# A two-stage kernel: q and k loaded by token, v's overlaps copied on chip, weights decoded two steps later

## The chip, the cores and the metric

The kernel runs on one core of one Trainium2 chip. The metric is the device time of one execution, in microseconds (us). The names used are TensorE (PE, with PEld for its weight loads), VectorE (DVE), ScalarE (ACT), GpSimd (POOL) and SyncE (SP, which issues all DMAs here).

## The reference, cut to what matters

```
attention, per batch and head (2 batches, 8 heads, 576 tokens, 64 wide, float32):
    scores = q @ k^T / 8
    heads 0-3: keep key j for query i if 0 <= i - j < 32
    heads 4-7: keep it if 0 <= i - j < 128 and (i - j) % 4 == 0
    attn = exp(scores - max) / (sum + 1e-9);  y = attn @ v
x = y as 1152 tokens x 512
x = mish(x @ w_in) @ w_out                          # 512 -> 2048 -> 512
out = sum over 4 experts e of p_e * (relu(x @ w1[e]) @ w2[e])   # 512 -> 1024 -> 512
```

## The kernel before, in words

**Units and steps.** The attention is cut into ten units, each a batch and a chunk of 128 tokens (the fifth chunk of a batch has 64), with all eight heads. `att_step(s)` (line 437) is a software pipeline over them: in step s it works on unit s+2 (`transposes`), s+1 (`spread`), s (`scores`, `softmax`, `probsT`), s-1 (`probsT_copy`, `values`, `sums`, `normalise`) and s-2 (`xT`, `x_hi`, `x_lo`). The schedule is manual: each engine runs its instructions in the order in which this function issues them, and so does SP with its DMAs. Steps run from -2 to 9.

**A unit's way.** `load_qk` (line 306) puts two tokens, 512 contiguous bytes, on a partition: the k of a unit on the first 64 partitions, the q on the other 64, one DMA each. `transposes` turns each head's block (line 320); `spread` (line 323) is eight ScalarE copies of 64 lanes x 256 that sort heads and even and odd tokens into `qkP` (heads 0 to 3) and `qkD` (heads 4 to 7). In these tiles k stands as head pairs: head j of a pair on partitions 64j to 64j+63, with zeros in the other half, so that one product gives the scores of two heads. `scores` adds the mask with a product of `sel` and `msk` and then runs products for 32 queries at a time (line 351) or for every fourth token (line 355). `softmax` is the row maximum `mx` (line 363), the subtraction `pr` (364) on VectorE and exp (365) on ScalarE; `sums` (369 to 371) are the row sums and their reciprocal; `normalise` (401) scales the outcome of `values` into `xn`. `xT` turns it, and `x_hi` (420, ScalarE) and `x_lo` (424, VectorE) split it into a high and a low part, xh and xl.

**v.** `vP` and `vD` hold v with the tokens of the block before on 32 of the 64 partitions of a head and the block's own tokens on the other 32. As blocks overlap, the DMAs of `load_vP` (260) and `load_vD` (273) read nearly every token twice. GpSimd zeroes the halves that belong to the other head of a pair (`zero_v`, 202, and `zero_k`, 214), chunk by chunk.

**Weights.** w_in and w_out are float32 and are needed as a high and a low part too. They come in 32 halves: half 2u is unit u's w_in (512 columns), half 2u+1 its w_out. A half is loaded into one of three `raw` buffers (`dec_load`), and then passes through five instructions, spread over three calls: `dec_dve` (143) with number n does line 150 of half n, line 157 of half n-1 and the GpSimd subtraction of line 164, which gives the low part, of half n-2; `dec_act` (167) does the conversion of line 173 of half n, writes the high part of half n-1 (line 179) and then counts n up. The first four units go to `wxh` and `wxl`, the others to the `late` tiles. In the attention steps there is one pair of calls per step, from `DEC0` on:

```
        if DEC0 <= s < NA:
            dec_act()
        if DEC0 - 4 <= s < DEC0 - 1:
            dec_load()
        if DEC0 - 1 <= s < NA:
            dec_dve()
```

After step 9 come two more `dec_act` and one `dec_dve`, written out by hand (lines 793 to 813), and then each of the steps 2 to 15 of the first matrix stage has two pairs (`step1_act`, 769).

**The matrix stages.** In stage one, step i multiplies the first 512 tokens by unit i of w_in (`first`, line 497, 12 products: per 128 rows of the weights high x xh, high x xl, low x xh), applies mish, splits, and multiplies by w_out (`second`, 517). For the sixteen steps of these tokens the order on TensorE is first(i), second(i-1), first(i+1), second(i), and on ScalarE in step i mish(i), the split into gh, and then the two `dec_act`. The other tokens and the four experts follow; all their operands are there by then or prepared beside them.

Of the kernel before, what the change touches and what calls it, by code (L numbers as in the profile page):

```python
# [8 lines left out]
F32 = mybir.dt.float32  # L9
# [5 lines left out]
AF = mybir.ActivationFunctionType  # L15
# [8 lines left out]
def kernel(  # L24
# [13 lines left out]
    PE, ACT, DVE, POOL, SP = nc.tensor, nc.scalar, nc.vector, nc.gpsimd, nc.sync  # L38
    ctx.enter_context(tc.manual_schedule())

    B, H, S, D = q.shape
# [3 lines left out]
    NF1 = w_in.shape[1] // 128  # L45
    NF2 = w1.shape[2] // 128
    NUA = 4
    DEC0 = 3
    NWARM = 8

    GRP = ((0, 512), (512, 320), (832, 320))
# [11 lines left out]
    def nm(s):  # L63
        uid[0] += 1
        return f"{s}{uid[0]}"

    def bank(n):
        return ps.tile([128, 512], F32, tag=f"bank{n}", name=nm("bank"))
# [120 lines left out]
    ap1 = att.enter_context(tc.tile_pool(name="ap1", bufs=1))  # L189
    NCH = (S + 127) // 128  # L190


    qkP = ap1.tile([128, 2, 3, 32 + S], F32, name="qkP")

    qkD = ap1.tile([128, 2, 3, NCH + 1, 2, 64], F32, name="qkD")
    vP = ap1.tile([128, 2, S // 32, 2, D], F32, name="vP")
    vD = ap1.tile([128, 2, 2, NCH, 4 * D], F32, name="vD")
    ident = ap1.tile([128, 128], F32, name="ident")
# [3 lines left out]
    def zero_v(c):  # L202
        blk = slice(4 * c, min(4 * c + 4, S // 32))
        for j in range(2):
            POOL.memset(vP[64 * j:64 * j + 64, :, blk, 1 - j, :], 0.0)  # L205
            if c == 0:
                POOL.memset(vP[64 * j:64 * j + 32, :, 0, j, :], 0.0)
        if c in (0, NCH - 1):
            POOL.memset(vD[:, :, :, c], 0.0)
        else:  # L210
            for j in range(2):
                POOL.memset(vD[64 * j:64 * j + 64, :, 1 - j, c], 0.0)  # L212

    def zero_k(c, eng):
        n = min(128, S - 128 * c)
        for j in range(2):
            rows = slice(64 * j, 64 * j + 64)
            eng.memset(qkP[rows, :, 1 - j, 32 + 128 * c:32 + 128 * c + n], 0.0)
            eng.memset(qkD[rows, :, 1 - j, c + 1, :, 0:n // 2], 0.0)

    warm = ap1.tile([128, 512], BF16, name="warm")
    DVE.memset(warm, 0.0)
# [9 lines left out]
                           base=-lo, pattern=[[1, 64]], channel_multiplier=-1 if lo == 0 else 0)  # L232
    for t in sel.values():
        DVE.memset(t, 0.0)
    DVE.memset(qkP[:, :, 0:2, 0:32], 0.0)
    for p in range(2):
        DVE.memset(qkD[:, p, 0:2, 0], 0.0)
        DVE.memset(qkD[:, p, 0:2, NCH, :, (S % 128) // 2:64], 0.0)
    zero_k(0, DVE)
    zero_v(0)  # L240
    for c in range(1, NCH):
# [10 lines left out]
    t = bank(7)  # L252
# [3 lines left out]
    def msk_b(n):  # L256
        return msk.unsqueeze(1).to_broadcast([64, n, 64])


    def load_vP(b, g0, g1):  # L260

        for j in range(2):
            src = v[b, j:j + 1]
            if g0 == 0:
                SP.dma_start(out=vP[64 * j + 32:64 * j + 64, :, 0, j, :],
                             in_=bass.AP(src.tensor, src.offset, [[D, 32], [2 * S * D, 2], [1, D]]))
            g = max(g0, 1)
            for p in range(2):
                SP.dma_start(out=vP[64 * j:64 * j + 64, p, g:g1, j, :],
                             in_=bass.AP(src.tensor, src.offset + (2 * p * S + 32 * (g - 1)) * D,  # L270
                                         [[D, 64], [32 * D, g1 - g], [1, D]]))

    def load_vD(b, c0, c1):

        for j in range(2):
            src = v[b, 4 + j:5 + j]
            lo, n = 64 * j, 64
            off = src.offset + 128 * (c0 - 1) * D
            if c0 == 0:
                lo, n, off = lo + 32, 32, src.offset  # L280
            elif c1 == NCH:
                n = 32 + (S - 128 * c0) // 4
            if c1 == c0 + 1:
                SP.dma_start(out=vD[lo:lo + n, :, j, c0, :],
                             in_=bass.AP(src.tensor, off, [[4 * D, n], [2 * S * D, 2], [1, 4 * D]]))
                continue
            for p in range(2):
                SP.dma_start(out=vD[lo:lo + n, p, j, c0:c1, :],
                             in_=bass.AP(src.tensor, off + 2 * p * S * D,
                                         [[4 * D, n], [128 * D, c1 - c0], [1, 4 * D]]))  # L290


    v_loads = {-2: [(load_vD, 0, 1, NCH - 1)], -1: [(load_vP, 0, 8, S // 32), (load_vD, 0, NCH - 1, NCH)],
               2: [(load_vD, 1, 0, 1), (load_vP, 1, 0, 8)], 4: [(load_vD, 1, 1, NCH - 1)],
               5: [(load_vP, 1, 8, S // 32), (load_vD, 1, NCH - 1, NCH)]}

    class Unit:
        def __init__(self, b, c):
# [5 lines left out]
            self.tbanks, self.sbank, self.s = ((4, 5), 6, None) if second else ((0, 1), 2, None)  # L304

        def load_qk(self):

            self.nat = ap1.tile([128, H, 2 * D], F32, tag="nat", name=nm("nat"), bufs=4)
            rows = slice(128 * self.c, 128 * self.c + self.n)
            for lo, src in ((0, k), (self.n // 2, q)):  # L310
                SP.dma_start(out=self.nat[lo:lo + self.n // 2],
                             in_=src[self.b, :, rows, :].rearrange("h (t two) d -> t h (two d)", two=2))

        def transposes(self):
            n = self.n
            self.pts = []
            for g in range(2):
                pt = bank(self.tbanks[g]).rearrange("p (h t) -> p h t", h=4)
                for h in range(4):
                    PE.transpose(pt[:, h, 0:n], self.nat[0:n, 4 * g + h, :], ident[0:n, 0:n])  # L320
                self.pts.append(pt[:, :, 0:n].rearrange("p (a j) (k t) -> p a j k t", j=2, k=2))

        def spread(self):

            n, c = self.n, self.c

            def move(g, par, j):
                src = slice(64 * par, 64 * par + 64)
                dst = slice(64 * j, 64 * j + 64)
                if g == 0:  # L330
                    cols = 32 + 128 * c
                    return qkP[dst, :, j:3:2 - j, cols + par:cols + n:2], self.pts[0][src, :, j]
                return qkD[dst, :, j:3:2 - j, c + 1, par, 0:n // 2], self.pts[1][src, :, j]

            for g in range(2):
                for par in range(2):
                    for j in range(2):
                        ACT.activation(*move(g, par, j), AF.Copy)  # L338

        def scores(self):  # L340
            n, c = self.n, self.c
            self.s = s = bank(self.sbank)
            if self.first:
                PE.matmul(s[:, 0:256], sel["s"], msk_b(4), start=True, stop=False, skip_group_check=True)
                PE.matmul(s[:, 256:512], sel["f"], msk_b(4), start=False, stop=False, skip_group_check=True)
            else:
                PE.matmul(s, sel["n"], msk_b(8), start=True, stop=False, skip_group_check=True)
            for p in range(2):
                for g in range(n // 32):
                    k0 = 128 * c + 32 * g  # L350
                    PE.matmul(s[32 * g:32 * g + 32, 128 * p:128 * p + 128], qkP[:, p, 2, k0 + 32:k0 + 64],
                              qkP[:, p, 0:2, k0:k0 + 64], start=False, stop=True, skip_group_check=True)
            for p in range(2):
                for r in range(4):
                    PE.matmul(s[32 * r:32 * r + n // 4, 256 + 128 * p:384 + 128 * p],
                              qkD[:, p, 2, c + 1, r % 2, r // 2:n // 2:2],
                              qkD[:, p, 0:2, c:c + 2, r % 2, r // 2::2], start=False, stop=True, skip_group_check=True)

        def softmax(self):
            mx = ap1.tile([128, 8], F32, tag="mx", name=nm("mx"), bufs=3)  # L360
# [12 lines left out]
        def probsT(self):  # L373
            pt = bank(3).rearrange("p (s t) -> p s t", s=4)
            pr = self.pr.rearrange("p s c -> p (s c)")
            for s in range(4):
                PE.transpose(pt[:, s, :], pr[:, 128 * s:128 * s + 128], ident)
            self.pt = pt

        def probsT_copy(self):  # L380
            self.pT = ap1.tile([128, 4, 128], F32, tag="pT", name=nm("pT"), bufs=1)
            ACT.activation(self.pT, self.pt, AF.Copy)

        def values(self):
            self.x = x = bank(4).rearrange("p (s d) -> p s d", s=4)
# [41 lines left out]
    NA = len(au)  # L427
    for n in range(3):
        au[n].load_qk()
    load_vP(0, 0, 8)  # L430
    load_vD(0, 0, 1)

    def unit_at(n):
        return au[n] if 0 <= n < NA else None
# [1 line left out]
    def att_step(s, mid=None, pre=None):  # L436
        n2, n1, u, p1, p2 = (unit_at(n) for n in (s + 2, s + 1, s, s - 1, s - 2))
        if p1:
            p1.probsT_copy()
        if n1:  # L440
            n1.spread()
        if pre:
# [7 lines left out]
        if p2:  # L450
            p2.xT()
        if p1:
            p1.sums()
        if p2:
            p2.x_hi()
            p2.x_lo()
        if DEC0 <= s < NA:
            dec_act()
        if p1:
            p1.normalise()  # L460
        if n2:
            n2.transposes()
        if mid:
# [2 lines left out]
            u.probsT()  # L466
        if unit_at(s + 5):
            unit_at(s + 5).load_qk()
        for load, *args in v_loads.get(s, ()):
            load(*args)  # L470
        if DEC0 - 4 <= s < DEC0 - 1:
            dec_load()
        if DEC0 - 1 <= s < NA:
            dec_dve()

    yacc = {}

# [315 lines left out]
    u1, u2 = au[NA - 1], au[NA - 2]  # L793
    ACT.preload_act_table_set(MISH)
    u1.probsT_copy()
    u1.values()
    u2.xT()
    steps[0].act()
    u1.sums()
    dec_act()  # L800
    dec_dve()
    steps[2].first()
# [108 lines left out]
```

## Time and profile before

| | us |
|---|---|
| median of 3 runs | 670.16 |
| lowest and highest run | 669.08, 671.54 |
| the profiled execution: time | 668.4 |
| the profiled execution: span from first to last instruction | 666.6 |
| TensorE, matmuls busy | 636.1 |
| VectorE busy | 290.3 |
| ScalarE busy | 275.3 |
| GpSimd busy | 158.8 |

The time of an execution is its span and the 1.8 us around it. The attention takes the first 75 us or so, the matrix stages the rest. Busy times of different engines overlap. A row of a timeline gives the start and the duration of an instruction, its line and operation, what it writes and reads, and in brackets how long its engine was idle before it and which instruction ended that wait.

### The profile page before, as it was taken

Reading aid. Unit: us, or ns where it says so; the run is one execution under the profiler, and the core shown is the slowest. Engines: PE = TensorE matmul, PEld = TensorE weight load, DVE = VectorE, ACT = ScalarE, POOL = GpSimd, SP = SyncE. Lnnn points to the kernel's source line nnn. Section 1 sums busy time; section 2 is a strip of 40 time slices with the busy share of each in tenths; the row PEclk is TensorE's granted clock in tenths of the full one; section 3 lists DMA queues with packets and bytes.
Section 4 is the critical chain, followed back from the end, with each engine's and each line's share of the span. In section 5 each row is a group of like instructions: output and inputs, shape, how many; then the busy total and the mean of one; then the engine's idle time right before and its main releaser. Section 6 shows DMA issues by size and latency. Waiting matters only on the chain.

```text
span 666.6 us, 10149 instructions
## 1 busy us (share of the span) xinstructions
PE 636.1 (95%) x4148; PEld 564.7 (85%) x4148; DVE 290.3 (44%) x490; ACT 275.3 (41%) x553; POOL 158.8 (24%) x170
## 2 busy tenths in 40 slices
PE   7676899999999999979999999999999999999997
PEld 4455678888999999969998889998889998898986
DVE  3577876661311223345444452444632544623323
ACT  7797666662322234443244432334422344322210
POOL 8011245550300003345033410043400134300000
PEclk9998999999999999989999999999999999999999
DMA  9999356640000012222003210021210022000102
GB/s 182 221 205 206 98 160 190 188 126 0 1 1 1 1 64 64 64 63 64 1 32 94 64 64 1 0 64 64 64 63 1 1 78 85 28 1 1 63 1 79
DMA packets 47310, 45.82 MB, mean 69 GB/s; under 512 B 12192, under 2 KB 39968, under 8 KB 47264
## 3 DMA queue, kind: packets, MB, share of 16 engines
q1 hardware_dynamic: 47264, 45.18, 25.6%
q8 instruction: 32, 0.52, 0.3%
q14 instruction: 14, 0.11, 0.1%
HBM read 42.81 MB, written 2.36 MB: 68 GB/s over the span
## 4 chain that ended last, share of the span: by engine, by line
PE 86%; ACT 4%; POOL 3%; DMA 2%; DVE 2%; issue 1%; SPq 0%; POOLq 0%; ACTq 0%; DVEq 0%
PE bank L751 30%; PE bank L698 27%; PE bank L517 14%; PE bank L497 14%; DMA raw<-in_moe_w_in_dram 1%; DMA nat<-in_q_dram 1%; ACT qkD L338 1%; ACT qkP L338 1%; ACT xh L420 1%; POOL vP L205 1%; POOL vD L212 0%; PE bank L320 0%; DVE xl L424 0%; DVE scr L150 0%; ACT pr L365 0%
## 5 line engine op out<-in xcount | busy, mean ns | idle before, releaser
L698 PE MATMUL bank<-xh,late 128*128 128x256 f32 (+1 forms) x512 | 121.1, 298 | 5.0 <-ACT late L710 3.6
L698 PEld LDWEIGHTS bank<-xh,late 128*128 128x128 f32 x512 | 88.6, 188 | 9.5 <-ACT late L710 5.1
L698 PE MATMUL bank<-wxh,late 128*128 128x320 f32 (+1 forms) x384 | 95.3, 298 | 0.0
L751 PE MATMUL bank<-late,gh 128*128 128x512 f32 x288 | 89.8, 393 | 0.0
L497 PE MATMUL bank<-xh,late 128*128 128x320 f32 (+1 forms) x288 | 76.3, 338 | 0.0
L698 PE MATMUL bank<-xl,late 128*128 128x256 f32 (+1 forms) x256 | 75.5, 295 | 0.0
L517 PE MATMUL bank<-gh,late 128*128 128x320 f32 (+1 forms) x288 | 72.6, 338 | 0.0
L654 POOL TENSOR_TENSOR raw<-raw 128x256 f32<-128x256 f32 x16 | 11.7, 734 | 238.4 <-DVE late L543 238.4
L698 PEld LDWEIGHTS bank<-wxh,late 128*128 128x128 f32 x384 | 68.3, 189 | 0.0
L506 DVE TENSOR_TENSOR gl<-scr,gh 128x512 fp32r<-128x512 f32 (+1 forms) x32 | 25.0, 780 | 88.7 <-ACT gh L505 88.7
L751 PEld LDWEIGHTS bank<-late,gh 128*128 128x128 f32 x288 | 52.8, 190 | 9.7
L502 ACT ACTIVATE scr<-bank 128x320 f32<-128x320 f32 (+1 forms) x48 | 23.4, 492 | 88.1 <-PE bank L497 88.1
L716 DVE TENSOR_TENSOR raw<-bank,late 128x256 f32<-128x256 f32 (+1 forms) x32 | 14.6, 457 | 101.2 <-PE bank L698 94.1
L751 PE MATMUL bank<-late,gl 128*128 128x512 f32 x144 | 57.0, 396 | 0.0
L698 PE MATMUL bank<-wxl,late 128*128 128x256 f32 (+1 forms) x192 | 56.6, 295 | 0.0
L542 ACT ACTIVATE late<-raw 128x512 fp32r<-128x512 f32 (+1 forms) x64 | 48.2, 783 | 19.9 <-PE bank L751 16.8
L497 PEld LDWEIGHTS bank<-xh,late 128*128 128x128 f32 x288 | 50.7, 188 | 4.3
L517 PEld LDWEIGHTS bank<-gh,late 128*128 128x128 f32 x288 | 50.1, 188 | 4.2
L751 PE MATMUL bank<-late,late 128*128 128x512 f32 x216 | 52.6, 391 | 0.0
L543 POOL TENSOR_TENSOR late<-raw,late 128x1024 fp32r<-128x1024 f32 x16 | 38.7, 2419 | 57.1 <-ACT late L542 57.1
L698 PEld LDWEIGHTS bank<-xl,late 128*128 128x128 f32 x256 | 48.3, 189 | 2.5
L497 PE MATMUL bank<-xl,late 128*128 128x320 f32 (+1 forms) x144 | 48.6, 338 | 0.0
(140 smaller groups left out, 1164.1 us busy)
## 6 DMA issues: line engine op xcount, KB each, us to landing
raw<-in_moe_w_dram SPq DMA_DIRECT2D x32, 512.0 KB, 3.5
raw<-in_moe_w_in_dram SPq DMA_DIRECT2D x16, 512.0 KB, 4.1
raw<-in_moe_w_out_dram SPq DMA_DIRECT2D x16, 512.0 KB, 3.6
out_dram<-scr SPq DMA_DIRECT2D x9, 256.0 KB, 2.1
nat<-in_k_dram SPq DMA_DIRECT2D x8, 256.0 KB, 5.6
nat<-in_q_dram SPq DMA_DIRECT2D x8, 256.0 KB, 6.2
vD<-in_v_dram SPq DMA_DIRECT2D x8, 192.0 KB, 7.0
vP<-in_v_dram SPq DMA_DIRECT2D x8, 160.0 KB, 6.5
```

The costliest lines, as they stand in the source:

```text
L205: POOL.memset(vP[64 * j:64 * j + 64, :, blk, 1 - j, :], 0.0)
L338: ACT.activation(*move(g, par, j), AF.Copy)
L497: PE.matmul(h, a[:, c, :], x[:, c, :], start=c == 0 and k == 0, stop=c == 3 and k == 2)
L502: ACT.activation(self.hc[:, self.w * i:self.w * (i + 1)], h, AF.Mish)
L506: DVE.tensor_tensor(out=self.glo, in0=self.hc, in1=self.ghi.bitcast(F32), op=ALU.subtract)
L517: PE.matmul(yacc[self.grp][d], a[:, s], x[:, g], start=u == 0 and k == 0, stop=u == NF1 - 1 and k == 2)
L542: ACT.activation(hi, src, AF.Copy)
L543: eng.tensor_tensor(out=lo, in0=src, in1=hi.bitcast(F32), op=ALU.subtract)
L654: POOL.tensor_tensor(out=a22, in0=a21, in1=a22, op=ALU.add)
L698: PE.matmul(out, w, x(k), start=first and k == 0 and i == 0, stop=k == 1 and i == 2, skip_group_check=not first)
L716: DVE.tensor_tensor(out=self.cb[:, 0:N], in0=self.c, in1=p1, op=ALU.add)
L751: PE.matmul(acc, x[:, s], a[:, cols], start=self.p == 0 and f == 0 and i == 0, stop=self.p == NP2 - 1 and f == 1 and i == 2)
```

## The change

- `load_qk` puts one token to a partition: a DMA for k and one for q, each 128 partitions x 8 heads x 256 bytes. A transpose of 128 columns is then a pair of heads, in place. `spread` becomes two copies of 64 lanes x 512 for k, with the zeros beside them, and one of 128 x 512 for q. `kk` and `qq` replace `qkP` and `qkD`; the dilated heads' products read every fourth token.
- `load_v` loads only a block's own tokens; `copy_v`, on GpSimd, copies those of the block before from there, in step s for unit s. The zeroing of `vD` for the first and the last chunk is cut into smaller pieces, so as to leave the loaded partitions out. v is loaded in two DMA groups for a batch in place of four.
- `DEC0` is 5 in place of 3.
- `sums` is issued at the start of a step, right after `probsT_copy`; `normalise` ahead of `x_hi` and `x_lo`.

```diff
-    DEC0 = 3
+    DEC0 = 5
...
-    qkP = ap1.tile([128, 2, 3, 32 + S], F32, name="qkP")
-    qkD = ap1.tile([128, 2, 3, NCH + 1, 2, 64], F32, name="qkD")
+    kk = ap1.tile([128, 4, 2, 128 * (NCH + 1)], F32, name="kk")
+    qq = ap1.tile([128, 4, S], F32, name="qq")
...
     def zero_v(c):
         blk = slice(4 * c, min(4 * c + 4, S // 32))
         for j in range(2):
             POOL.memset(vP[64 * j:64 * j + 64, :, blk, 1 - j, :], 0.0)
+            POOL.memset(vD[64 * j:64 * j + 64, :, 1 - j, c], 0.0)
             if c == 0:
                 POOL.memset(vP[64 * j:64 * j + 32, :, 0, j, :], 0.0)
-        if c in (0, NCH - 1):
-            POOL.memset(vD[:, :, :, c], 0.0)
-        else:
-            for j in range(2):
-                POOL.memset(vD[64 * j:64 * j + 64, :, 1 - j, c], 0.0)
+                POOL.memset(vD[64 * j:64 * j + 32, :, j, 0], 0.0)
+            if c == NCH - 1:
+                POOL.memset(vD[64 * j + 32:64 * j + 64, :, j, c], 0.0)
     def zero_k(c, eng):
-        n = min(128, S - 128 * c)
         for j in range(2):
-            rows = slice(64 * j, 64 * j + 64)
-            eng.memset(qkP[rows, :, 1 - j, 32 + 128 * c:32 + 128 * c + n], 0.0)
-            eng.memset(qkD[rows, :, 1 - j, c + 1, :, 0:n // 2], 0.0)
+            eng.memset(kk[64 * j:64 * j + 64, :, 1 - j, 128 * c + 128:128 * c + 256], 0.0)
...
+    def load_v(b, c0, c1):
+        g0, g1 = 4 * c0, min(4 * c1, S // 32)
+        cf = min(c1, S // 128)
         for j in range(2):
+            own = slice(64 * j + 32, 64 * j + 64)
             for p in range(2):
+                src = v[b, 2 * p + j:2 * p + j + 1]
+                SP.dma_start(out=vP[own, p, g0:g1, j, :],
+                             in_=bass.AP(src.tensor, src.offset + 32 * g0 * D, [[D, 32], [32 * D, g1 - g0], [1, D]]))
+            src = v[b, 4 + j:5 + j]
+            for p in range(2):
+                SP.dma_start(out=vD[own, p, j, c0:cf, :],
+                             in_=bass.AP(src.tensor, src.offset + (2 * p * S + 128 * c0) * D,
+                                         [[4 * D, 32], [128 * D, cf - c0], [1, 4 * D]]))
+            if cf < c1:
+                n = (S - 128 * cf) // 4
+                SP.dma_start(out=vD[64 * j + 32:64 * j + 32 + n, :, j, cf, :],
...
+    def copy_v(c):
+        g0, g1 = max(4 * c, 1), min(4 * c + 4, S // 32)
         for j in range(2):
+            before, own = slice(64 * j, 64 * j + 32), slice(64 * j + 32, 64 * j + 64)
+            POOL.tensor_copy(vP[before, :, g0:g1, j, :], vP[own, :, g0 - 1:g1 - 1, j, :])
+            if c:
+                POOL.tensor_copy(vD[before, :, j, c, :], vD[own, :, j, c - 1, :])
+    v_loads = {-2: (0, 2, NCH), 3: (1, 0, 2), 5: (1, 2, NCH)}
...
         def load_qk(self):
-            self.nat = ap1.tile([128, H, 2 * D], F32, tag="nat", name=nm("nat"), bufs=4)
             rows = slice(128 * self.c, 128 * self.c + self.n)
-            for lo, src in ((0, k), (self.n // 2, q)):
-                SP.dma_start(out=self.nat[lo:lo + self.n // 2],
-                             in_=src[self.b, :, rows, :].rearrange("h (t two) d -> t h (two d)", two=2))
+            self.nat = []
+            for x in "kq":
+                t = ap1.tile([128, H, D], F32, tag="nat" + x, name=nm("nat" + x), bufs=4)
+                SP.dma_start(out=t[0:self.n], in_=(k if x == "k" else q)[self.b, :, rows, :].rearrange("h t d -> t h d"))
+                self.nat.append(t.rearrange("p h d -> p (h d)"))
...
         def spread(self):
+            n, t0 = self.n, 128 * self.c
+            for j in range(2):
+                rows = slice(64 * j, 64 * j + 64)
+                ACT.activation(kk[rows, :, j, 128 + t0:128 + t0 + n], self.pt[0][rows], AF.Copy)
+            ACT.activation(qq[:, :, t0:t0 + n], self.pt[1], AF.Copy)
...
-                              qkD[:, p, 2, c + 1, r % 2, r // 2:n // 2:2],
-                              qkD[:, p, 0:2, c:c + 2, r % 2, r // 2::2], start=False, stop=True, skip_group_check=True)
+                              qq[:, 2 + p, t0 + r:t0 + n:4], kk[:, 2 + p, :, t0 + r:t0 + 256:4],
+                              start=False, stop=True, skip_group_check=True)
...
-    load_vP(0, 0, 8)
-    load_vD(0, 0, 1)
+    load_v(0, 0, 2)
...
         if p1:
             p1.probsT_copy()
+            p1.sums()
+        if u:
+            copy_v(u.c)
         if n1:
             n1.spread()
...
         if p1:
-            p1.sums()
+            p1.normalise()
         if p2:
             p2.x_hi()
             p2.x_lo()
         if DEC0 <= s < NA:
             dec_act()
-        if p1:
-            p1.normalise()
```

## Rows read from the trace of the kernel before

**Rows 1.** Busy time by stretch: PE, PEld, DVE, ACT, POOL, clock, DMA share, GB/s.

```profile
20.00:40.00 20.00, 14.82 (x271) 11.16 (x269) 12.72 (x27) 16.21 (x40) 0.11 (x1) 1.00 1.15 219
...
84.80:163.00 78.20, 78.20 (x344) 63.89 (x345) 43.08 (x61) 44.27 (x73) 33.83 (x24) 1.00 0.46 141
```

**Rows 2.** Chain of waits, 56 to 66 us: start, duration, what.

```profile
56.51 0.43 DVE scr L150
...
58.90 0.63 ACT pr L365
...
59.55 0.91 ACT xh L420 x2
...
60.48 0.99 DVE xl L424 x2
61.48 0.56 DVE xn L401
...
62.09 1.07 DVE scr L150
63.16 0.60 DVE scr L157
63.76 0.61 DVE mx L363
...
64.39 0.70 DVE pr L364
...
65.12 0.63 ACT pr L365
```

**Rows 3.** Timeline of ScalarE: the exp of the last unit.

```profile
71.36 0.63 ACT L365 ACTIVATE pr<-pr 128x512 f32<-128x512 f32 x1 [2.53 <-DVE pr L364]
```

**Rows 4.** DMA view of two stretches: 5 to 8 us, and 20 to 22.5 us.

```profile
DMA packets 1270, 0.63 MB, mean 211 GB/s; under 512 B 34, under 2 KB 1270, under 8 KB 1270
...
DMA packets 1630, 0.43 MB, mean 172 GB/s; under 512 B 1552, under 2 KB 1630, under 8 KB 1630
```

**Rows 5.** Groups of ScalarE up to 84 us, by shape: count, busy us, mean ns.

```profile
L338 ACT ACTIVATE qkP<-bank 64x256 f32<-64x256 f32 x32 | 12.9, 403 | 3.1 <-PE bank L320 2.8
...
L382 ACT ACTIVATE pT<-bank 128x512 f32<-128x512 f32 x10 | 6.0, 598 | 3.1 <-PE bank L377 3.1
```

**Rows 6.** Timeline of TensorE: the dilated score products of a unit.

```profile
39.26 0.64 PE L355 MATMUL bank<-qkD 128*32 128x128 f32 x16
```

**Rows 7.** Groups of VectorE, 56 to 72 us: the row sums and the reciprocal.

```profile
L369 DVE TENSOR_REDUCE sm<-pr 128x8 f32<-128x512 f32 x3 | 2.0, 675 | 0.0
...
L371 DVE RECIPROCAL sm<-sm 128x8 f32<-128x8 f32 x2 | 0.4, 203 | 0.1
```

**Rows 8.** Timeline of GpSimd: the last memsets.

```profile
14.69 0.52 POOL L212 MEMSET vD<- 64x512 f32 x1
...
16.73 0.96 POOL L209 MEMSET vD<- 128x1024 f32 x1
17.63 0.17 POOL L245 MEMSET raw<- 128x2 uint32 x3
```

**Rows 9.** Timeline of TensorE: transposes of the second unit.

```profile
8.63 1.72 PE L320 MATMUL bank<-ident,nat 128*128 128x128 f32 x8 [0.60 <-DMA nat<-in_q_dram]
```

**Rows 10.** Timelines of GpSimd and of the weight loads, in two places.

```profile
109.29 1.59 POOL L164 TENSOR_TENSOR late<-scr,late 128x512 fp32r<-128x512 f32 x1 [2.76 <-ACT late L179]
...
109.63 0.19 PEld L497 LDWEIGHTS bank<-xh,late 128*128 128x128 f32 x1
...
77.45 1.73 POOL L164 TENSOR_TENSOR wxl<-scr,wxh 128x512 fp32r<-128x512 f32 x1 [2.27 <-ACT wxh L179]
...
77.53 0.19 PEld L497 LDWEIGHTS bank<-xh,wxl 128*128 128x128 f32 x1
```

**Rows 11.** Line 164: ns at least, median, at most; first and last start.

```profile
L164 POOL TENSOR_TENSOR late<-scr,late x24: 1287/1302/1724, 86.4 to 149.8; 128x512 fp32r<-128x512 f32 x24
```

**Rows 12.** Line 497 from 92 to 160 us: products that read xh.

```profile
L497 PE MATMUL bank<-xh,late x96: 392/396/399, 92.6 to 156.8; 128*128 128x512 f32 x96
```

More of the change, by code (lines that the diff above doesn't have):

```diff
@@ L234 @@
         DVE.memset(t, 0.0)
[L235 to L238, printed above, removed]
+    for j in range(2):
+        DVE.memset(kk[:, :, j, 0:128], 0.0)
+        DVE.memset(kk[:, 2:4, j, 128 + S:], 0.0)
     zero_k(0, DVE)
@@ L257, in msk_b @@
         return msk.unsqueeze(1).to_broadcast([64, n, 64])
-    def load_vP(b, g0, g1):
+    def load_v(b, c0, c1):
+        g0, g1 = 4 * c0, min(4 * c1, S // 32)
+        cf = min(c1, S // 128)
         for j in range(2):
[L263 to L267, printed above, removed]
-            for p in range(2):
-                SP.dma_start(out=vP[64 * j:64 * j + 64, p, g:g1, j, :],
-                             in_=bass.AP(src.tensor, src.offset + (2 * p * S + 32 * (g - 1)) * D,
-                                         [[D, 64], [32 * D, g1 - g], [1, D]]))
@@ L273, in load_vD @@
-    def load_vD(b, c0, c1):
-        for j in range(2):
[L276 to L290, printed above, removed]
@@ L293 @@
-    v_loads = {-2: [(load_vD, 0, 1, NCH - 1)], -1: [(load_vP, 0, 8, S // 32), (load_vD, 0, NCH - 1, NCH)],
-               2: [(load_vD, 1, 0, 1), (load_vP, 1, 0, 8)], 4: [(load_vD, 1, 1, NCH - 1)],
-               5: [(load_vP, 1, 8, S // 32), (load_vD, 1, NCH - 1, NCH)]}
+            own = slice(64 * j + 32, 64 * j + 64)
+            for p in range(2):
+                src = v[b, 2 * p + j:2 * p + j + 1]
+                SP.dma_start(out=vP[own, p, g0:g1, j, :],
+                             in_=bass.AP(src.tensor, src.offset + 32 * g0 * D, [[D, 32], [32 * D, g1 - g0], [1, D]]))
@@ new lines, in load_v @@
+            src = v[b, 4 + j:5 + j]
[6 more added lines that the diff above has]
+                SP.dma_start(out=vD[64 * j + 32:64 * j + 32 + n, :, j, cf, :],
+                             in_=bass.AP(src.tensor, src.offset + 128 * cf * D, [[4 * D, n], [2 * S * D, 2], [1, 4 * D]]))
@@ L314, in transposes @@
         def transposes(self):
             n = self.n
[L316 to L321, printed above, removed]
-        def spread(self):
[L325 to L338, printed above, removed]
+            self.pt = []
@@ new lines, in transposes @@
+            for x, nat in enumerate(self.nat):
+                pt = bank(self.tbanks[x]).rearrange("p (a t) -> p a t", a=4)[:, :, 0:n]
+                for a in range(4):
+                    PE.transpose(pt[:, a], nat[0:n, 128 * a:128 * a + 128], ident[0:n, 0:n])
+                self.pt.append(pt)
+        def spread(self):
+            n, t0 = self.n, 128 * self.c
+            for j in range(2):
+                rows = slice(64 * j, 64 * j + 64)
+                ACT.activation(kk[rows, :, j, 128 + t0:128 + t0 + n], self.pt[0][rows], AF.Copy)
+            ACT.activation(qq[:, :, t0:t0 + n], self.pt[1], AF.Copy)
@@ L347, in scores @@
                 PE.matmul(s, sel["n"], msk_b(8), start=True, stop=False, skip_group_check=True)
+            t0 = 128 * c
             for p in range(2):
                 for g in range(n // 32):
-                    k0 = 128 * c + 32 * g
-                    PE.matmul(s[32 * g:32 * g + 32, 128 * p:128 * p + 128], qkP[:, p, 2, k0 + 32:k0 + 64],
-                              qkP[:, p, 0:2, k0:k0 + 64], start=False, stop=True, skip_group_check=True)
+                    t = t0 + 32 * g
+                    PE.matmul(s[32 * g:32 * g + 32, 128 * p:128 * p + 128], qq[:, p, t:t + 32],
+                              kk[:, p, :, t + 96:t + 160], start=False, stop=True, skip_group_check=True)
             for p in range(2):
@@ L377, in probsT @@
                 PE.transpose(pt[:, s, :], pr[:, 128 * s:128 * s + 128], ident)
-            self.pt = pt
+            self.prT = pt
         def probsT_copy(self):
             self.pT = ap1.tile([128, 4, 128], F32, tag="pT", name=nm("pT"), bufs=1)
-            ACT.activation(self.pT, self.pt, AF.Copy)
+            ACT.activation(self.pT, self.prT, AF.Copy)
         def values(self):
@@ L468, in att_step @@
             unit_at(s + 5).load_qk()
-        for load, *args in v_loads.get(s, ()):
-            load(*args)
+        if s in v_loads:
+            load_v(*v_loads[s])
         if DEC0 - 4 <= s < DEC0 - 1:
@@ L795 @@
     u1.probsT_copy()
+    u1.sums()
     u1.values()
@@ L798 @@
     steps[0].act()
-    u1.sums()
     dec_act()
```

## The prediction

> **What bounds the kernel now.** The chain of waits of the whole execution is nearly all TensorE, but that is an average over two stages, so I asked first for the engines' busy time by stretch. From 84.8 us on TensorE has no idle time: 78.2 us busy in 78.2 [rows 1], and nothing behind that waits for the attention. What the attention stage before it takes is therefore handed on one for one: a microsecond gained there is a microsecond gained at the end, as long as TensorE, once it is full, stays full. Before 84.8 no engine is full (20 to 40 us: TensorE 14.8 of 20, VectorE 12.7, ScalarE 16.2), while the DMA share is over 1 [rows 1].
>
> The chain of the attention's late steps says what sets their period [rows 2]: exp of a unit, x_hi, x_lo, xn, the two decode operations of lines 150 and 157, the next unit's mx and pr, and exp again, from 58.90 to 65.12, that is 6.22 us. All but exp and x_hi are VectorE's queue, in program order. The line-150 shift takes 0.43 alone and 1.07 when GpSimd is busy. The last exp starts at 71.36 [rows 3].
>
> **The change, part by part.**
>
> *Loads.* q and k (4.72 MB) go from pieces of 512 B to 256 B. What a byte costs is read in two stretches in which nearly all packets have one size: 211 GB/s where they are 512 B, 172 where 1552 of 1630 are under 512 B (the vP loads) [rows 4]. So a unit's k and q, 0.524 MB, take 3.05 us, not 2.48, and all nine units' worth 27.4, not 22.4: 5.0 more. v is moved once in place of nearly twice: the pieces of 256 B fall from 2.29 to 1.18 MB, which at 172 GB/s saves 6.5, those of 1024 B from 2.23 to 1.18 MB, which at 211 saves 5.0. The number of DMA issues on SP is the same, 18 per batch. Net: 6.5 us less transfer, and three weight loads move from steps -1 to 1 to steps 1 to 3, out of the most crowded part. What the end sees of this is bounded by the loop below.
>
> The Trainium skill ("DMA: Bandwidth & Descriptors", Specifications) speaks against this part: it wants at least 512 B for line rate, since smaller pieces cost a read-modify-write. The trace agrees only in part: the loss is 18%.
>
> *Spreading k and q.* Eight ScalarE copies of 64x256 at 0.40 become three; a copy of 512 elements a lane takes 0.60 [rows 5], so 1.8 in place of 3.2 us a step. ScalarE is not on the late loop while it copies, so I cost this at nothing beyond letting the early steps run at the loop's period. The dilated products of line 355 now step through memory by 16 bytes, not 8; no row shows that step. Sixteen of them take 0.64 now [rows 6]; I take no change, and a doubling, 0.6 a step, would still lie beside VectorE's loop.
>
> *The order on VectorE.* normalise (xn, 0.56) leaves the loop: it now stands in the gap in which VectorE waits for exp and x_hi. sums enter it, ahead of mx: 0.68 and two small ones of 0.20 [rows 7], 1.05 in all. GpSimd's subtraction, beside which line 150 took 1.07, starts after ScalarE's second conversion; with xn gone, line 150 comes 0.6 earlier and should run alone, 0.43. Loop with decode: 6.22 - 0.56 + 1.05 - 0.64 = 6.07. Without decode (steps up to 3 now, 1 before): 6.07 - 0.43 - 0.60 = 5.0.
>
> *Copies of v on GpSimd.* They stand behind all zeroing in GpSimd's queue. That ends at 17.8 now; two memsets of 0.96 become eight of 0.52 [rows 8], 2.2 more; the zeroing of k has as many elements as before. So the copies start near 20.0, and unit 0's two (384 elements) end near 21.2. Price of one: no copy is in the trace; between a memset of 512 (0.52) and a subtraction with two inputs (1.29, [rows 11]), I take 0.6 to 0.8, because a copy has one input. Before, nothing of this stood ahead of the values of unit 0, and TensorE takes its queue in order: behind those values wait the transposes of unit 3, the probabilities of unit 1 and the scores of unit 2. Unit 3 itself has landed: the second unit landed at 8.63 [rows 9], plus 2 x 0.57, two more units (6.1) and 0.52 MB of v (3.0) gives 18.9. Charging one period after 21.2 puts the exp of unit 2 at about 26.5. Later, four copies of 0.8 and one subtraction of 1.3 per step fit in 6.07.
>
> *Sum for the attention.* exp of unit 2 at 26.5, units 3 and 4 after 5.0 each, unit 5 after 5.43 (line 150 alone), units 6 to 9 after 6.07 each: 66.2, against 71.36. Gain 5.2. Ends: if copies cost little and the early wait vanishes, 8; if line 150 still meets GpSimd each time (4 x 0.64) and the copies cost 1.3 each, a loss of 2.
>
> *Weights decoded later.* This is the part that I expect to decide. Two dec_act calls fall away, and the order of all that follows is fixed by the program. Before, seven dec_act calls ran by the end of step 9, now five. In step1_act(i) the two calls then convert n = 2i+3 and 2i+4 (before 2i+5 and 2i+6), and dec_act(n) writes the high part of half n-1. So the high part of half 2i+2, the w_in of unit i+1, is written in the first call of step1_act(i), and its low part in the dec_dve after that; before, both were done a whole step earlier. steps[i+1].first, which reads them, is the very next on TensorE but one.
>
> The trace shows when that slot is. In the step at 106.8 GpSimd's subtraction starts at 109.29 and takes 1.59, to 110.88; TensorE's third weight load of the next first, which is the first to read the low part, is at 109.63 [rows 10]. It would have to wait until about 110.96: 1.33 us. The slot follows first(i) by fixed work on ScalarE (mish, gh, conversion, high part), so nothing catches up, and the wait returns at each step: firsts of units 4 to 15, twelve of them (96 products that read xh, eight to a first), which come without idle time now [rows 12]. 12 x 1.33 = 16.0. Ends: the subtraction takes 1.287 at least and 1.724 at most [rows 11], so 1.03 to 1.46, 12.3 to 17.6. The first time it bites is steps[2].first: its half 4 would be in the slot at 77.45 to 79.18, where the third weight load is at 77.53 [rows 10]: 1.7 more, or 0.5 if a later wait swallows part. What is queued behind the waiting weight load is all of TensorE. Decode stage: +17.7, between 12.8 and 19.6.
>
> *Sum.* 17.7 - 5.2 = +12.5 on the profiled execution: its span 666.6, its time 668.4, which is 1.8 under the median of 670.16. 668.4 becomes 680.9; on the median, 682.7. I say 683.
>
> **The rivals.**
>
> *The lag is one half, not two.* If the decode had one half more in hand than I count, the low part would come in the second slot of the step before and no weight load would wait: the point is 109.63, and the subtraction would have ended 2 us earlier or more. That leaves the attention's gain alone: 670.2 - 5.2 = 665, faster. For it speaks only that the count is mine; against it that line 179 first writes late tiles (half 8) in step1_act(2), just as the same count gives for the kernel before. 5%. The wait could also be matched by more gain than I allow, with the early wait gone and shorter loops: 13 of gain against 13 of wait, about 670. 6%.
>
> *Small pieces at half rate.* With q and k at half of 211 GB/s, not 172, their transfer takes 44.7 us, not 27.4. The last of v waits behind all of it: 44.7, and 6.9 for the small pieces of v, 13.0 for its large ones and three weight loads, and some 3 before anything lands, is 68. Its copies and two steps put the last exp near 77.5, 6 later than now: 670.2 + 17.7 + 6 = 694. The vP loads, whose pieces are 256 B already, speak against it [rows 4]. 5%. This is where the Trainium skill's rule ("DMA: Bandwidth & Descriptors", Specifications) would lead.
>
> *GpSimd becomes the bound.* Four copies of 1.29 and a subtraction of 1.29 are 6.45 a step, over the loop's 6.07, and early on 5.2 a step against 5.0; with values waiting for copies throughout, the gain goes: 670.2 + 17.7 = 688. 9%.
>
> **How the numbers follow.** My forecast, 683, has 75%. Its own bounds: 670.2 + 12.8 - 8 = 675 and 670.2 + 19.6 + 2 = 692. The range 673 to 692 holds that and the third rival, and leaves out the first and the half-rate case. About 0.5%, or 3.4 us, is what a measurement of this kernel can tell from no change. Faster by more than that: 5%. Within it: 6%. Slower: 89%.
>
> **What would show it.** Right: twelve idle times of 1.0 to 1.5 us of the weight loads of line 497, released by GpSimd's line 164, with first-to-first at about 6.9 in place of 5.6; the last exp near 66; values of unit 0 waiting for a GpSimd copy until about 21; sums between line 157 and mx in the chain. Wrong: the products of line 497 and 517 still without gaps after 93 us, which fells the sum's largest term; or a last exp outside 63 to 73; or pieces of 256 B moving far below 172 GB/s.

## The result and the profile after

The change makes the kernel slower: 681.16 us in the median of four runs, against 670.85 for four runs of the kernel before beside it, a ratio of 1.0148 (95% interval 1.012 to 1.0176). The forecast was 683, in a range of 673 to 692. The profiled execution took 681.41, its span is 679.6, 13.0 more than before; the medians differ by 10.3, as the profiled execution before, 668.4, lay below its median.

The page of the changed kernel, busy time of TensorE and the chain that ended last by engine:

```profile
span 679.6 us, 10142 instructions
...
PE 644.4 (95%) x4148; PEld 565.1 (83%) x4148; DVE 294.2 (43%) x487; ACT 261.5 (38%) x503; POOL 180.9 (27%) x204
...
PE 80%; ACT 6%; DVE 5%; POOL 4%; issue 2%; DMA 1%; SPq 0%; POOLq 0%; DVEq 0%; ACTq 0%
```

Where the 13.0 us come from is read at three marks. The exp of the last unit, at 71.36 before [rows 3], is at 68.81: the attention gained 2.55. The first product of steps[4].first, the first that reads a late tile, at 92.64 before (92.6 in [rows 12]), is at 91.90, only 0.74 earlier. The first product of the next group of tokens moved from 159.8 to 172.7, 12.9 later. The rows of the last two marks on TensorE's timeline, first before, then after:

```profile
92.64 0.40 PE L497 MATMUL bank<-xh,late 128*128 128x512 f32 x1
...
159.79 0.31 PE L497 MATMUL bank<-xh,wxh 128*128 128x320 f32 x1
```

```profile
91.90 0.45 PE L480 MATMUL bank<-xh,late 128*128 128x512 f32 x1
...
172.68 0.31 PE L480 MATMUL bank<-xh,wxh 128*128 128x320 f32 x1
```

So 13.6 us are lost between these two marks, over twelve firsts. The view of waits from 80 to 180 us, for the weight loads and for the products (total us, times, longest):

```profile
PEld bank L480 <- POOL late L164: 15.6, 12, 1.3
...
PE bank L480 <- POOL late L164: 10.4, 12, 0.9
```

Line 480 is `first`, line 497 before. Before, the products of line 497 had no idle time from 92 to 160 us. The chain of waits through two of these steps (start, duration, what):

```profile
98.61 1.58 POOL late L164
...
100.23 2.61 PE bank L480 x10
...
102.87 0.61 ACT scr L485
...
103.50 0.63 ACT gh L488
104.13 0.68 ACT scr L173
104.81 0.48 ACT late L179
...
105.36 1.58 POOL late L164
...
106.98 2.61 PE bank L480 x10
```

It is a closed loop: a first ends, ScalarE runs mish, the split, a conversion and the high part, GpSimd subtracts, and the third product of the next first may begin. It comes round in 6.75 us (98.61 to 105.36), where a step took 5.60 before. The weight loads and the subtraction in the place of [rows 10]:

```profile
98.70 0.19 PEld L480 LDWEIGHTS bank<-xl,late 128*128 128x128 f32 x1
100.23 0.30 PEld L480 LDWEIGHTS bank<-xh,late 128*128 128x128 f32 x2 [1.35 <-POOL late L164]
```

In the attention two things stand out. First, unit 0's values wait for the copies behind the zeroing; GpSimd's row, TensorE's row and the busy time by stretch (PE, PEld, DVE, ACT, POOL, clock, DMA share, GB/s):

```profile
19.32 0.18 POOL L240 MEMSET raw<- 128x2 uint32 x3
19.42 1.72 POOL L281 COPY vP<-vP 32x384 f32<-32x384 f32 x3
```

```profile
20.53 0.86 PE L371 MATMUL bank<-vP,pT 128*32 128x128 f32 x11 [5.53 <-POOL vP L281]
```

```profile
15.40:20.50 5.10, 0.00 (x0) 0.00 (x0) 0.00 (x0) 1.33 (x3) 4.72 (x13) 0.56 0.34 64
20.50:28.00 7.50, 7.47 (x99) 5.96 (x103) 2.21 (x5) 2.27 (x4) 7.13 (x13) 0.61 0.84 172
```

TensorE does nothing for 5.1 us, and then it is busy almost without a gap for 7.5 us at a granted clock of 0.61 of its 2.4 GHz: from 20.5 to 26.0 us it is 0.50, the lower level of 1.2 GHz. Second, the exps, on ScalarE's timeline, and one decode operation of VectorE beside GpSimd's subtraction:

```profile
16.13 0.62 ACT L347 ACTIVATE pr<-pr 128x512 f32<-128x512 f32 x1
...
29.06 0.63 ACT L347 ACTIVATE pr<-pr 128x512 f32<-128x512 f32 x1 [1.45 <-DVE pr L346]
33.83 0.63 ACT L347 ACTIVATE pr<-pr 128x512 f32<-128x512 f32 x1 [1.67 <-DVE pr L346]
38.59 0.63 ACT L347 ACTIVATE pr<-pr 128x512 f32<-128x512 f32 x1 [1.02 <-DVE pr L346]
43.70 0.63 ACT L347 ACTIVATE pr<-pr 128x512 f32<-128x512 f32 x1 [1.38 <-DVE pr L346]
49.44 0.63 ACT L347 ACTIVATE pr<-pr 128x512 f32<-128x512 f32 x1 [1.61 <-DVE pr L346]
54.84 0.63 ACT L347 ACTIVATE pr<-pr 128x512 f32<-128x512 f32 x1 [1.10 <-DVE pr L346]
61.93 0.63 ACT L347 ACTIVATE pr<-pr 128x512 f32<-128x512 f32 x1 [3.08 <-DVE pr L346]
68.81 0.63 ACT L347 ACTIVATE pr<-pr 128x512 f32<-128x512 f32 x1 [3.92 <-DVE pr L346]
```

```profile
64.28 0.43 DVE L150 TENSOR_SCALAR scr<-raw 128x512 uint32<-128x512 uint32 x1
64.61 1.80 DVE L157 SCALAR_TENSOR_TENSOR scr<-raw,scr 128x512 uint32<-128x512 uint32 x1
```

```profile
64.53 1.33 POOL L164 TENSOR_TENSOR wxl<-scr,wxh 128x512 fp32r<-128x512 f32 x1 [2.98 <-issue]
```

From unit 1 to unit 2 the exps are 12.9 us apart; then 4.8, 4.8 and 5.1 without line 157, 5.7 and 5.4 with it, and 7.1 and 6.9 where it starts just behind the subtraction and takes 1.8 in place of 0.7.

### The profile page after: what moved, and what is told of

The parts are those of the page before. It is cut to its first block, busy times and chain, and to the rows that moved or that the text cites. A ratio compares the mean times of both kernels' runs of the same rounds, so it can differ in the third digit from the quotient of the medians.

```text
span 679.6 us, 10142 instructions
## 1 busy us (share of the span) xinstructions
PE 644.4 (95%) x4148; PEld 565.1 (83%) x4148; DVE 294.2 (43%) x487; ACT 261.5 (38%) x503; POOL 180.9 (27%) x204
## 4 chain that ended last, share of the span: by engine, by line
PE 80%; ACT 6%; DVE 5%; POOL 4%; issue 2%; DMA 1%; SPq 0%; POOLq 0%; DVEq 0%; ACTq 0%
PE bank L734 29%; PE bank L681 26%; PE bank L480 14%; PE bank L500 9%; POOL late L164 3%; ACT scr L173 1%; ACT scr L485 1%; ACT gh L488 1%; DVE scr L157 1%; DVE pr L346 1%; ACT late L179 1%; DVE mx L345 1%; ACT xh L402 1%; DMA natq<-in_q_dram 1%; DVE xl L406 1%
## 5 line engine op out<-in xcount | busy, mean ns | idle before, releaser
L480 PEld LDWEIGHTS bank<-xh,late 128*128 128x128 f32 x288 | 49.6, 188 | 20.1 <-POOL late L164 15.6
L500 PE MATMUL bank<-gl,late 128*128 128x320 f32 (+1 forms) x144 | 48.6, 337 | 0.0
```

The costliest lines, as they stand in the source:

```text
L480: PE.matmul(h, a[:, c, :], x[:, c, :], start=c == 0 and k == 0, stop=c == 3 and k == 2)
L500: PE.matmul(yacc[self.grp][d], a[:, s], x[:, g], start=u == 0 and k == 0, stop=u == NF1 - 1 and k == 2)
```

## The experiments

Ten kernels ran, each beside the kernel before, whose median was 671.01 in the first four, 671.35 in the next four and 670.82 in the last two. A ratio is the time divided by that of the kernel before, with its 95% interval in brackets. "Less than the change" compares with 681.16. Marks such as the last exp are read from one execution of each kernel.

### The low part read last

```diff
-                for c in range(4):
-                    for k, (a, x) in enumerate(((wh, vh), (wh, vl), (wl, vh))):
-                        PE.matmul(h, a[:, c, :], x[:, c, :], start=c == 0 and k == 0, stop=c == 3 and k == 2)
+                todo = [(a, x, c) for c in range(4) for a, x in ((wh, vh), (wh, vl))] + [(wl, vh, c) for c in range(4)]
+                for k, (a, x, c) in enumerate(todo):
+                    PE.matmul(h, a[:, c, :], x[:, c, :], start=k == 0, stop=k == 11)
```

> The changed kernel, but in each first of line 480 the four products that read a weight's low part come last instead of every third. Nothing of the decode moves. Theory (the low part of half 2i+2 is late by 1.15 us for TensorE, twelve times): it is now read 8 products, 1.9 us, after the first one, so the twelve waits for GpSimd's subtraction and the one of steps[2].first go, 12 x 1.14 + 0.7 = 14.4 us; 667, between 666 and 669. Rival (what is late is the chain of ScalarE and VectorE behind mish, the subtraction only its last link, so that the wait returns elsewhere): 676 or more, with TensorE waiting for ScalarE instead.

Measured: 666.1 us, ratio 0.9932 (0.9912 to 0.9953), 15.1 less than the changed kernel. Busy time by stretch in this run:

```profile
90.00:176.00 86.00, 85.36 (x405) 70.81 (x403) 43.55 (x62) 47.85 (x83) 36.92 (x26) 1.00 0.41 128
```

TensorE is full again; its queue does not wait for GpSimd in this stage, though the decode runs as late as in the change: GpSimd's subtraction starts 0.1 before a first does, in both. The stretch between the two marks of the result, with its twelve firsts, takes 67.2 us in place of 80.8, 13.6 less. So the wait was for the low part alone, and nothing took its place. The rival falls. Some 1.3 of the 15.1 may have nothing to do with the edit: the last exp is at 67.51 in this execution, with the attention's code as in the change.

### DEC0 = 4

```diff
-    DEC0 = 5
+    DEC0 = 4
```

> The changed kernel with DEC0 = 4. Theory (the order of the calls decides): the high part of half 2i+2 is then written in the second call of step1_act(i-1), the low part ends some 2.5 us before it is read, no weight load waits: 13.7 less for the twelve firsts, up to 1 more for one more decode step in the attention; 667 to 669. Rival (the lag has to be two whole calls, one leaves half of the wait): 674.

Measured: 669.25 us, ratio 0.9972 (0.9946 to 0.9998), 11.9 less than the change. The waits for GpSimd are gone, but the last exp is at 71.48, 2.67 later than with DEC0 = 5: one more decode step was dearer than the 1 us allowed, and 669.25 is just past the end of what was expected. The stretch between the marks takes 67.1 us, as before the change. One call of lead is enough; the rival falls.

### The later decode in the kernel before

```diff
-    DEC0 = 3
+    DEC0 = 5
```

> The kernel before with DEC0 = 5 alone. Theory: the twelve waits appear here too, 13.7, and the one of steps[2].first, up to 1.5; against it two attention steps without decode, each 0 to 1 shorter: 670.9 + 14 - 1 = 684, between 681 and 686. Rival (the loss belongs to the new loads and copies, by GpSimd's and VectorE's contention): 670 or a little less.

Measured: 682.24 us, ratio 1.0173 (1.0135 to 1.0211), 11.2 more than its own comparison. The waits from 80 to 180 us are those of the changed kernel:

```profile
PEld bank L497 <- POOL late L164: 15.6, 12, 1.4
...
PE bank L497 <- POOL late L164: 10.3, 12, 0.9
```

The last exp is at 69.82, 1.54 earlier than before. With the loads, copies and order of the kernel before, this one number makes a loss as large as that of the whole change.

### The zeroing of k on VectorE

```diff
     for c in range(1, NCH):
-        zero_k(c, POOL)
+        zero_k(c, DVE)
         zero_v(c)
```

> The changed kernel with the zeroing of k for chunks 1 to 4, eight memsets of 64 x 512, on VectorE instead of GpSimd. Theory (unit 0's values wait for copies that stand behind all zeroing): the copies start about 4.3 us earlier, TensorE's idle time of 5.1 us at 15.4 shrinks to about 1, and its clock does not fall to 0.6 behind it, 4 to 6.5 us in all: 675 to 677. Rival (v lands too late for that, or the gain is swallowed by a later wait): 680 or more.

Measured: 676.12 us, ratio 1.0085 (1.0053 to 1.0117), 5.0 less than the change. The chain of waits and the busy time, to be held against 19.42, 20.53 and the clock of 0.61:

```profile
15.00 0.43 POOL vP L281
...
16.04 0.53 PE bank L371 x11
...
21.90 0.63 ACT pr L347
```

```profile
15.00:28.00 13.00, 11.61 (x203) 9.09 (x204) 7.76 (x15) 7.77 (x17) 9.87 (x19) 1.00 1.02 200
```

The values of unit 0 run 4.5 us earlier (16.04 against 20.53), and the exp of unit 2 comes 7.2 us earlier: 4.5 for the wait, and 2.7 less from these values to that exp, in which the clock now stays at 1.00. Of the 7.2, 5.4 are left at the last exp (63.37).

### sums ahead of normalise

```diff
             p1.probsT_copy()
-            p1.sums()
...
         if p1:
+            p1.sums()
             p1.normalise()
```

> The changed kernel with sums issued right ahead of normalise, in the gap in which VectorE waits for exp and x_hi, instead of at the start of the step. Theory (VectorE's queue is the loop of the decode steps, and sums stand on it with 1.0 us): the four steps with line 157 get shorter by 0.5 to 1.0 each, those without decode hardly, as TensorE's own work is about 4.7 of their 4.77; 681.2 - 2.8 = 678.4, between 677 and 680. Rival (these steps are set by GpSimd's lock, which line 157 waits out, and sums stand in its shadow): 681.

Measured: 679.02 us, ratio 1.0109 (1.0084 to 1.0135), 2.1 less than the change. The last exp is at 65.87, 2.9 earlier, of which 0.6 are there already at the exp of unit 2 (28.48). Of the four steps with line 157 three are shorter, by 0.5 to 0.8, and one is 0.3 longer. A gain of this sign and near this size was expected, and the time lies clear of the rival's 681 (the highest of four runs is 679.72); that sums stand on the loop holds.

### All edits, with DEC0 = 4 and 5

The diffs above on the low part, the zeroing of k and sums together, once with this edit and once without it:

```diff
-    DEC0 = 5
+    DEC0 = 4
```

> The changed kernel with four edits: DEC0 = 4, the low part's products last in first, the zeroing of k on VectorE, sums ahead of normalise. Theory (the three costs are independent and add): 676.1 - 14.4 - 2.8 + 1.5 for one more decode step = 660.5, between 658 and 663. Rival (what is gained in the attention is taken back by the waits for weights and v): 664 or more.

> As the run with four edits, but DEC0 = 5. Theory (with the low part read late, the later decode costs nothing and spares a decode step of the attention): 659, 1 to 2.7 less than with DEC0 = 4. Rival (the later decode still costs in the first matrix stage): 662 or more.

Measured: 660.82 us with DEC0 = 4, ratio 0.9841 (0.9802 to 0.9881), and 661.38 with DEC0 = 5, ratio 0.9847 (0.9824 to 0.987). Both beat the kernel before by about 10 us, and the three costs add as expected in the first. The second expectation missed: DEC0 = 5 is not faster. Its last exp is only 0.65 earlier (62.16 against 62.81), and nothing of that reaches the end. The traces show where it goes: from the last exp to steps[4].first 22.7 us pass, against 21.3 with DEC0 = 4, and from 66 to 74 us TensorE's granted clock is 0.75 and then 0.82 (4 us each), where the other run has 1.00; the stretch with the twelve firsts takes 67.7 against 67.1. Why the clock falls there was not tried. Once its cost in the firsts is removed, the later decode has nothing measurable left to give.

### DEC0 = 3: all of the change but the later decode

```diff
-    DEC0 = 5
+    DEC0 = 3
```

> The changed kernel with DEC0 = 3, that is all of the change but the later decode. Theory: no wait for the low part, as with DEC0 = 4, and one more decode step in the attention, which costs 1 to 2.7; 671, between 669.5 and 672, so that the new loads, copies and order by themselves give nothing against the kernel before. Rival (decode steps are free beside the attention's other waits): 669 or less.

Measured: 671.95 us, ratio 0.9999 (0.9981 to 1.0018). New loads, copies and order together give nothing and cost nothing that can be measured; what separates the change from the kernel before is the later decode. The two halves of the attention cancel: the exp of unit 2 is at 27.65, 3.7 later than before (23.97), and from there to the last exp it takes 43.3 us in place of 47.4. The same stretch takes 39.75 with DEC0 = 5 and 42.4 with DEC0 = 4, so in these executions the first of two more decode steps costs 2.6 and the second 0.95.

### The new loads without copies, and the copies alone

The first is the changed kernel with DEC0 = 3 and all that concerns v as before; the second is the kernel before with all that concerns v, its zeroing too, as in the change:

```diff
-    load_v(0, 0, 2)
+    load_vP(0, 0, 8)
+    load_vD(0, 0, 1)
...
-        if u:
-            copy_v(u.c)
```

```diff
-    load_vP(0, 0, 8)
-    load_vD(0, 0, 1)
+    load_v(0, 0, 2)
...
+        if u:
+            copy_v(u.c)
```

> The changed kernel with DEC0 = 3 and with v's zeroing and loads as in the kernel before, overlaps from memory, no copies: the new q and k loads and the new order on VectorE alone. Theory (small pieces cost transfer time, 5.0 us more, and v's double loading 11.5 more than in the change; the front is bound by transfers): the early wait and the low clock go, but the middle steps wait for q, k and weights; last exp at 72 to 76, 674, between 672 and 676. Rival (it is the copies on GpSimd that cost, by the early wait and the lock): 668 or less.

> The kernel before with v loaded once and copied by GpSimd, and its zeroing, as in the change; q and k, VectorE's order and DEC0 = 3 as before. Theory (transfers 11.5 us less, but unit 0's values wait until about 21 for the copies): the exp of unit 2 at 27 to 29, no waits for weights after it, steps of 6.2 set by ScalarE and VectorE; last exp near 70.5, 670, between 668 and 672. Rival (copies meet VectorE's decode operations at every step): 675 or more.

Measured: 672.82 us for the loads without copies, ratio 1.0026 (1.0005 to 1.0046), and 669.42 for the copies alone, ratio 0.9967 (0.9949 to 0.9986). Both times lie in the ranges of the theories. Without copies the exp of unit 2 is at 22.13, but later VectorE waits for weights, four times and 10.3 us in all; the two longest waits on its timeline in that run:

```profile
29.18 0.43 DVE L150 TENSOR_SCALAR scr<-raw 128x512 uint32<-128x512 uint32 x1 [4.57 <-DMA raw<-in_moe_w_in_dram]
...
49.85 0.43 DVE L150 TENSOR_SCALAR scr<-raw 128x512 uint32<-128x512 uint32 x1 [2.84 <-DMA raw<-in_moe_w_out_dram]
```

and the last exp is at 74.76. The kernel before has four such waits too, 6.7 us in all. With the copies alone the exp of unit 2 is at 29.35, no operation of line 150 waits for a DMA in the attention, and the last exp is at 72.26. So the double loading of v costs transfer time in the middle and the copies cost a late start, and here they weigh about the same, to within some 2 us. One premise of the first theory does not hold: in its first 60 us this run moves 12.0 MB at 200 GB/s, the kernel before 12.1 at 201, so no loss of rate by the smaller pieces shows. Why its last exp is 3.4 later than before even so is not shown in full; its last two steps are 7.1 and 6.9 us, where before they were 6.2.

## Why the prediction was right, step by step

**The sum.** It forecast +12.5 on the profiled execution, and +13.0 came (10.3 in the medians). That the sum came so near is partly luck: its two terms were each too large by about 2.5 us, with opposite signs.

**Weights decoded later: forecast +17.7, measured about 15.4.** The mechanism, the place and the number of waits were right: twelve, each released by line 164, and three experiments show that they make the loss (low part read last, DEC0 = 4, the kernel before with 5). The weight load waits 1.30 on the mean (15.6 for twelve; 1.35 in the place shown), near the 1.33 of the forecast. But the step "12 x 1.33" took the wait of the weight load for that of the path: it runs ahead of the products, so that only the longer period counts, 6.75 - 5.60 = 1.15, and twelve such are 13.8 (13.6 between the marks). What stands between the last exp and steps[4].first cost 1.8 (23.1 us against 21.3), for which 1.7 had been put down to half 4's low part. That term was mis-sized: in the run with the low part read last nothing waits for it there, and the stretch is still 22.6. So the low part made some 0.5 of the 1.8, in these two executions, the lower figure that the prediction gave. The rest goes with a low clock: 0.56 from 74.4 to 77.9 us in the change, 0.66 from 73 to 77 in that run, and 1.00 before. What brings the clock down there was not tried.

**Attention: forecast a gain of 5.2, measured 2.55.** The 2.55 is of single executions; the run with the low part read last, with the same attention, would give 3.85. The whole shortfall of the profiled execution is there at the exp of unit 2, 2.6 late. From there on the sum was met, 39.75 against 39.7, but by two errors that cancel: units 3 to 5 were 0.8 faster than forecast, units 6 to 9 0.8 slower. Of its steps:

*The early wait* was placed rightly: copies of 0.6, ended at 20.5 where 21.2 was forecast. The step that failed is "one period after 21.2 puts the exp of unit 2 at about 26.5": it came at 29.06. TensorE had been idle for 5.1 us, and then ran at a clock of 0.61 until 28. The prediction had no term for the clock. The run with the zeroing of k on VectorE, where TensorE waits 1.4 us there and the clock stays at 1.00, shows 2.7 us on top of the wait. The other runs with this wait bear it out: unit 0's values start at 20.5 in all, and with a clock of 0.60, 0.61, 0.70, 0.73 and 0.81 from 20.5 to 28 us the exp of unit 2 comes at 29.12 (DEC0 = 4), 29.06 (the change), 28.48 (sums moved), 28.27 (low part last) and 27.65 (DEC0 = 3). So the clock's share differs from execution to execution.

*The order on VectorE.* "line 150 should run alone, 0.43" came true, and the loop without line 157 was 4.8 (5.0 forecast). But the step left line 157 out: in the steps of units 8 and 9 it starts 0.3 us later beside the subtraction and takes 1.80. The steps with this meeting are 7.1 and 6.9, not 6.07; the two without it 5.7 and 5.4. The Trainium skill ("SBUF — State Buffer", Who interferes with whom) has a VectorE instruction with two inputs in SBUF contend with a GpSimd instruction that reads SBUF, and the later one block fully. The trace agrees: line 157 starts 0.08 after the subtraction, which ends at 65.86, and ends at 66.41, 0.55 behind it. In the run with the low part read last, whose attention is that of the change, the meeting goes once each way:

```profile
57.10 1.96 POOL L164 TENSOR_TENSOR wxl<-scr,wxh 128x512 fp32r<-128x512 f32 x1 [1.74 <-issue]
57.23 0.68 DVE L157 SCALAR_TENSOR_TENSOR scr<-raw,scr 128x512 uint32<-128x512 uint32 x1
...
63.26 1.31 POOL L164 TENSOR_TENSOR wxl<-scr,wxh 128x512 fp32r<-128x512 f32 x1 [1.76 <-PE bank L359]
63.31 1.81 DVE L157 SCALAR_TENSOR_TENSOR scr<-raw,scr 128x512 uint32<-128x512 uint32 x1
```

Each time one of the two takes as long as both together would, though the first pair shows that it need not be the one whose row starts later. Where the subtraction is the one that waits, the step of unit 8 is 6.14 us, against 7.09 in the change: the meeting costs the loop about 0.95. No run took it away on purpose.

*Loads.* The price of the small pieces was wrong, without harm. The DMA view of the changed kernel, 5 to 8 us, nearly all k and q:

```profile
DMA packets 2581, 0.65 MB, mean 216 GB/s; under 512 B 2581, under 2 KB 2581, under 8 KB 2581
```

Pieces of 256 B move at 216 GB/s here, not at the 172 of the vP loads [rows 4], and not below the 211 of the pieces of 512 B. The 5.0 us "more" were not there, and what the Trainium skill ("DMA: Bandwidth & Descriptors", Specifications) says of pieces under 512 B does not show in these loads at all. Why the vP loads were slower wasn't tried. The end gained nothing by the loads: with them but without the copies the kernel takes 2.0 us more than the kernel before, and with DEC0 = 3 as much as it.

**The rivals.** "The lag is one half, not two" describes what DEC0 = 4 does, and no weight load waits there, as the rival's point said; the change itself is at two. GpSimd did not become the bound: its copies take 0.6, not 1.29. The half rate did not come.

## What to carry to other kernels

When work is postponed in a schedule written out by hand, count for each of its results how many calls lie between the one that writes it and the one that reads it; a lead that falls to nothing costs a wait at every later step of the loop, not once, and that loop is found by following one result from the engine that frees it to the engine that reads it. Before giving lead back, look whether the reader can take the late operand last: the same four products at the end of a group hid twelve waits that cost 13.6 us of 681. A queue's first piece of real work should not stand behind all of its preparation, and the price of such a wait includes the low clock after it.

## What was not expected of the hardware

After 5.1 us without work TensorE was granted 0.61 of its clock over the next 7.5 us, though it was busy for 7.47 of them; in four more runs with the same wait it was between 0.60 and 0.81, and the next exp moved by 1.5 us with it. Beside GpSimd's subtraction, VectorE's line 157 took 1.8 us in place of 0.7, or the subtraction 1.96 in place of 1.3. And pieces of 256 B on 128 partitions moved at 216 GB/s, where others of the same size, written to 64 partitions, had moved at 172.
